# Hand-written order, a first batch on three queues, and q transposed by DMA, in a linear-attention and bilinear-FFN kernel

## The chip, the cores and the metric

The kernel runs on one core of one Trainium2 chip. The metric is the device time of one execution in microseconds (us). Every time quoted is the median of several runs. The span of a profile, from the first to the last instruction, is about 1.8 us shorter than the time of the same run; where spans and times are set beside each other, the text says so.

The engines are named as the profile names them: PE or TensorE (matmuls), PEld (its weight loads), DVE (VectorE), ACT (ScalarE), POOL (GpSimd), SP (the engine that here only issues transfers).

## The reference

Linear attention without a softmax, an RMS norm of each head's output, and then a bilinear feed-forward layer (FFN):

```python
# q, k, v: (8 batches, 8 heads, 576 tokens, 64), fp32; g_norm: (64,)
kv  = np.einsum('bhsd,bhse->bhde', k, v)
out = np.einsum('bhsd,bhde->bhse', q, kv)
rms = np.sqrt(np.mean(out * out, axis=-1, keepdims=True) + 1e-06)
x   = (out / rms * g_norm).transpose(0, 2, 1, 3).reshape(4608, 512)
# w_a, w_b: (512, 1536); w_out: (1536, 512)
result = ((x @ w_a) * (x @ w_b)) @ w_out          # (4608, 512), fp32
```

The kernels do all matmuls in bf16.

## The kernel before

A batch's attention makes 576 columns of `xt`, the transposed x. The FFN then eats `xt` in nine strips of 512 tokens. The attention of batch s+1 is woven into strip s. Only batches 0 and 1 have no earlier strip to hide in, which is why the first 75 us of the kernel differ from the rest.

All loads of q, k and v are issued by POOL and cast to bf16 in flight. DVE then reorders k and q so that TensorE can read them, and TensorE transposes q, five transposes to each of four pairs of heads:

```python
        def qT(self, p):                       # one pair of heads
            qt = self.t["qr"]                  # q, reordered by DVE
            ps = apsum.tile([128, S], BF16, name="q_ps", tag="at")
            for c in range(NCH + 1):           # 4 chunks of 128 tokens and one of 64
                nc.tensor.transpose(ps[:, c*128 : c*128+r], qt[0:r, c, hs, :], ident[0:r, 0:r])
            qs = asb_pool.tile([128, S], BF16, name="qs", tag="qs", bufs=5)
            nc.vector.tensor_copy(qs, ps)
        def xu(self, p, h):                    # x product of half h of the tokens, then its square
            ps = apsum.tile([128, HF], FP32, name="x_ps", tag="at")
            nc.tensor.matmul(ps, lhsT=self.kvd[:, p, :], rhs=self.qs[p][:, h*HF:(h+1)*HF], ...)
            nc.scalar.activation(sq, ps, AF.Square)
        def ss(self, p, h):                    # sum of squares, 1/rms, and the column of xt
            ps = apsum.tile([128, HF], FP32, name="s_ps", tag="at")
            nc.tensor.matmul(ps, lhsT=ones, rhs=self.sq[p, h], start=True, stop=True)
            nc.scalar.activation(rs, ps, AF.Abs_reciprocal_sqrt, bias=eps_t)
            nc.vector.scalar_tensor_tensor(out=xt[p][...], in0=self.x_ps[p, h],
                                           scalar=g_col, in1=rs, op0=ALU.mult, op1=ALU.mult)
# ... (kv products, loads)
    def ffn_ab(s, fc):                         # one of 12 units of a strip: 8 matmuls
        # 4 matmuls into a_ps, 4 into b_ps, 512 columns each
        nc.scalar.copy(a_sb, a_ps)
        nc.vector.tensor_mul(t, b_ps, a_sb)
# ... ffn_o: 4 groups of 12 output matmuls to each strip, then a store
    drain(Attn(0, loaded.pop(0), 2).slices())
    for fc in range(FC):
        ffn_ab(0, fc)
    drain(Attn(1, loaded.pop(1), 2).slices())
    for s in range(1, N_STRIP): ...            # strip s with the attention of batch s+1 woven in
```

(Cuts are marked with "..." here and in the code below.) There are four PSUM buffers under the tag "at", which kv, q, x and s share in turn, and four under the tag "f" for the FFN. An automatic scheduler chooses the final order on every engine.

## Time and profile before

| | before |
|---|---|
| time, median of 4 runs | 369.06 us (368.75 to 371.54) |
| span of the profiled run (its time: 371.11 us) | 369.4 us |
| period of a strip in the steady part | 36.9 us (strips 1 to 3), 37.1 us (strips 4 to 6) |
| end of batch 0's attention | 28.9 us |
| last a or b product of strip 0 ends | 56.7 us |

The profile cuts the span into 40 equal slices. A digit is the busy share of a slice in tenths; for PEclk it is the granted TensorE clock in tenths of full speed. These are three rows of the page of the kernel before:

```profile
PE   0588859999999999999999999999999999999994
...
PEclk9999885699999999999999999999999999999998
...
DMA  8999999999901511151001111100001111101023
```

TensorE is busy for 90% or more of every slice from the seventh to the last but one, but at full clock only from the ninth on (74 us). Until 102 us the transfers are full. The clock row reads 9 wherever the trace has no clock record, and the first record of this trace comes at 26.0 us. The matmuls tell the truth there: the 512-column ones took 631 ns before 25.5 us and 378 ns after 26 us. From 64 to 70 us, where the record reads 0.50, they took 631 ns again, so the 512-column matmuls before the first record ran at half clock.

Next, the table of stretches, of the kernel before. Its columns are the window, its length, the busy time of PE, PEld, DVE, ACT and POOL (with counts), the granted clock, the DMA share (the packets' times added up, over 16 engines: it passes 1 where packets overlap) and GB/s.

```profile
50.00:60.00 10.00, 5.77 (x33) 3.11 (x32) 3.77 (x7) 1.41 (x5) 3.97 (x6) 0.66 1.57 192
60.00:70.00 10.00, 8.95 (x37) 3.93 (x36) 5.49 (x13) 6.32 (x17) 5.41 (x7) 0.50 1.58 192
74.10:111.00 36.90, 36.90 (x202) 18.21 (x202) 18.05 (x32) 16.44 (x39) 8.14 (x10) 1.00 1.16 158
```

The last row is one period of the steady part: TensorE is busy in all of its 36.9 us, at full clock, and DVE and ACT in under half. There, only work taken off TensorE can help. The groups of instructions, by form, show what the transposes of q are. The columns are the count, the busy time, the mean ns of one, and the idle time before.

```profile
L175 DVE COPY qs<-q_ps 128x576 bf16<-128x576 bf16 x32 | 14.5, 452 | 13.9 <-PE q_ps L171 13.9
L171 PE MATMUL q_ps<-ident,qr 128*128 128x128 bf16 x128 | 14.3, 241 | 0.0
...
L171 PE MATMUL q_ps<-ident,qr 64*128 64x64 bf16 x32 | 6.7, 209 | 0.0
```

In the timeline of the start, TensorE stands twice before an FFN product. The bracket gives the idle time and what ended it.

```profile
38.41 0.38 PE L233 MATMUL b_ps<-xt_122,wb_t 128*128 128x512 bf16 x1 [2.17 <-DVE abt L243]
...
53.30 0.69 DVE L126 COPY kr<-kt 128x2048 bf16<-128x2048 bf16 x1 [6.21 <-DMA kt<-in_k_dram]
...
54.12 1.27 DVE L243 TENSOR_TENSOR abt<-b_ps,a_sb 128x512 bf16<-128x512 f32 x2
...
54.84 0.59 PE L233 MATMUL b_ps<-xt_122,wb_t 128*128 128x512 bf16 x1 [4.23 <-DVE abt L243]
```

The scheduler had put the reorder of a later batch's k (53.30) ahead of the product that TensorE needed (54.12), and that reorder waited 6.21 us for its load; the product ran only after it.

### The profile page before, as it was taken

Reading aid. Unit: us, or ns where it says so; the run is one execution under the profiler, and the core shown is the slowest. Engines: PE = TensorE matmul, PEld = TensorE weight load, DVE = VectorE, ACT = ScalarE, POOL = GpSimd, SP = SyncE. Lnnn points to the kernel's source line nnn. Section 1 sums busy time; section 2 is a strip of 40 time slices with the busy share of each in tenths; the row PEclk is TensorE's granted clock in tenths of the full one; section 3 lists DMA queues with packets and bytes.
Section 4 is the critical chain, followed back from the end, with each engine's and each line's share of the span. In section 5 each row is a group of like instructions: output and inputs, shape, how many; then the busy total and the mean of one; then the engine's idle time right before and its main releaser. Section 6 shows DMA issues by size and latency. Waiting matters only on the chain.

```text
span 369.4 us, 4627 instructions
## 1 busy us (share of the span) xinstructions
PE 341.7 (93%) x1744; PEld 163.8 (44%) x1744; DVE 149.7 (41%) x268; ACT 140.2 (38%) x320; POOL 57.6 (16%) x80
## 2 busy tenths in 40 slices
PE   0588859999999999999999999999999999999994
PEld 0333324444444444445444444444444444444441
DVE  1343535545543554355434543354335432222310
ACT  1164113633562356235523552355235522132210
POOL 7955635535000200020000000000000000000000
PEclk9999885699999999999999999999999999999998
DMA  8999999999901511151001111100001111101023
GB/s 96 177 196 192 165 193 192 191 191 204 210 32 30 69 51 31 29 73 49 28 30 28 28 30 29 30 28 29 30 28 30 28 28 30 29 28 59 28 58 85
DMA packets 51414, 28.61 MB, mean 77 GB/s; under 512 B 14528, under 2 KB 46784, under 8 KB 51392
## 3 DMA queue, kind: packets, MB, share of 16 engines
q0 software_dynamic: 45728, 18.88, 41.5%
q1 hardware_dynamic: 5664, 9.44, 9.2%
q8 instruction: 13, 0.21, 0.3%
q14 instruction: 9, 0.07, 0.1%
HBM read 37.75 MB, written 9.44 MB: 128 GB/s over the span
## 4 chain that ended last, share of the span: by engine, by line
PE 81%; DMA 11%; POOL 3%; ACT 2%; DVE 1%; issue 1%; POOLq 0%; ACTq 0%; DVEq 0%
PE o_ps L269 26%; PE a_ps L233 23%; PE b_ps L233 22%; DMA kt<-in_k_dram 4%; PE kv_ps L154 3%; PE q_ps L171 3%; DMA wa_t<-in_moe_w_a_dram 3%; DMA qt<-in_q_dram 2%; PE s_ps L194 2%; DMA vt<-in_v_dram 2%; PE x_ps L180 2%; POOL wb_t L67 1%; POOL wa_t L66 1%; ACT rs L196 1%; ACT sq L188 0%
## 5 line engine op out<-in xcount | busy, mean ns | idle before, releaser
L243 DVE TENSOR_TENSOR abt<-b_ps,a_sb 128x512 bf16<-128x512 f32 x108 | 74.4, 691 | 100.7 <-PE b_ps L233 94.2
L241 ACT CAST a_sb<-a_ps 128x512 bf16<-128x512 f32 x108 | 63.1, 586 | 108.1 <-PE a_ps L233 106.5
L269 PE MATMUL o_ps<-wo_t,abt 128*128 128x512 bf16 x432 | 98.6, 379 | 0.0
L233 PEld LDWEIGHTS <-wb_t 128*128 128x128 bf16 x432 | 42.8, 99 | 60.6 <-issue 13.3
L269 PEld LDWEIGHTS <-abt 128*128 128x128 bf16 x432 | 41.3, 98 | 46.7
L233 PEld LDWEIGHTS <-wa_t 128*128 128x128 bf16 x432 | 39.9, 99 | 39.0 <-issue 2.4
L233 PE MATMUL b_ps<-xt_122,wb_t 128*128 128x512 bf16 x108 | 42.4, 393 | 6.4 <-DVE abt L243 6.4
L233 PE MATMUL a_ps<-xt_122,wa_t 128*128 128x512 bf16 x108 | 42.6, 394 | 0.0
L233 PE MATMUL a_ps<-xt_123,wa_t 128*128 128x512 bf16 x108 | 41.9, 388 | 0.0
L233 PE MATMUL a_ps<-xt_125,wa_t 128*128 128x512 bf16 x108 | 41.2, 381 | 0.7 <-DVE xt_125 L198 0.5
L233 PE MATMUL b_ps<-xt_123,wb_t 128*128 128x512 bf16 x108 | 41.8, 387 | 0.0
L233 PE MATMUL b_ps<-xt_125,wb_t 128*128 128x512 bf16 x108 | 41.4, 384 | 0.0
L233 PE MATMUL b_ps<-xt_124,wb_t 128*128 128x512 bf16 x108 | 41.4, 384 | 0.0
L233 PE MATMUL a_ps<-xt_124,wa_t 128*128 128x512 bf16 x108 | 41.2, 381 | 0.2 <-DVE xt_124 L198 0.2
L188 ACT ACTIVATE sq<-x_ps 128x288 bf16<-128x288 f32 x64 | 26.1, 411 | 33.2 <-PE x_ps L180 32.8
L196 ACT ACTIVATE rs<-s_ps,eps_t 128x288 f32<-128x288 f32 x64 | 31.7, 498 | 1.9 <-PE s_ps L194 1.7
L154 PE MATMUL kv_ps<-vt,kr 128*128 128x128 bf16 (+1 forms) x160 | 20.2, 241 | 13.0 <-DMA vt<-in_v_dram 12.0
L280 DVE COPY o_sb<-o_ps 128x512 f32<-128x512 f32 x18 | 12.5, 692 | 38.3 <-PE o_ps L269 38.3
L278 ACT COPY o_sb<-o_ps 128x512 f32<-128x512 f32 x18 | 10.5, 586 | 45.4 <-PE o_ps L269 45.4
L154 PEld LDWEIGHTS <-kr 128*128 128x128 bf16 (+1 forms) x160 | 13.9, 105 | 24.4 <-issue 6.9
L86 POOL DMA_DIRECT2D vt<-in_v_dram x10 | 9.4, 941 | 77.1 <-PE kv_ps L154 71.6
L194 PE MATMUL s_ps<-sq,ones 128*128 128x288 bf16 x64 | 19.7, 308 | 1.8 <-ACT rs L196 0.7
(42 smaller groups left out, 196.4 us busy)
## 6 DMA issues: line engine op xcount, KB each, us to landing
out_dram<-o_sb SPq DMA_DIRECT2D x40, 128.0 KB, 2.4
out_dram<-o_sb SPq DMA_DIRECT2D x16, 256.0 KB, 2.2
kt<-in_k_dram POOLq DMA_DIRECT2D x6, 512.0 KB, 12.6
vt<-in_v_dram POOLq DMA_DIRECT2D x6, 512.0 KB, 10.7
qt<-in_q_dram POOLq DMA_DIRECT2D x6, 512.0 KB, 12.4
wa_t<-in_moe_w_a_dram POOLq DMA_DIRECT2D x6, 256.0 KB, 8.4
wb_t<-in_moe_w_b_dram POOLq DMA_DIRECT2D x6, 256.0 KB, 9.0
wo_t<-in_moe_w_out_dram POOLq DMA_DIRECT2D x2, 768.0 KB, 9.7
```

Of the source, the lines that this page charges most:

```text
L86: nc.gpsimd.dma_start(out=t[:, hs, 0:NCH, :], in_=src[b, hs, 0:SA, :].rearrange("h (sp c) d -> sp h c d", c=NCH),)
L154: nc.tensor.matmul(self.kv_ps[:, p, :], lhsT=kt[0:r, c, hs, :], rhs=vt[0:r, hs, c, :], start=(c == 0), stop=(c == NCH),)
L171: nc.tensor.transpose(ps[:, c * 128 : c * 128 + r], qt[0:r, c, hs, :], ident[0:r, 0:r])
L188: nc.scalar.activation(sq, ps, AF.Square)
L194: nc.tensor.matmul(ps, lhsT=ones, rhs=self.sq[p, h], start=True, stop=True)
L196: nc.scalar.activation(rs, ps, AF.Abs_reciprocal_sqrt, bias=eps_t)
L233: nc.tensor.matmul(ps, lhsT=w[:, kc, fc * 128 : (fc + 1) * 128], rhs=xt[kc][:, t0 : t0 + STRIP], start=(kc == 0), stop=(kc == KC - 1),)
L241: nc.scalar.copy(a_sb, a_ps)
L243: nc.vector.tensor_mul(t, b_ps, a_sb)
L269: nc.tensor.matmul(o_ps, lhsT=ab[s, fc][:, g * 128 : (g + 1) * 128], rhs=wo_t[:, fc, :], start=(fc == 0), stop=(fc == FC - 1),)
L278: nc.scalar.copy(o_sb, o_ps)
L280: nc.vector.tensor_copy(o_sb, o_ps)
```

## The change

Its intent: the scheduler is switched off and all engines run in the written order. The first batch's k and q arrive as fp32 on the queues of SP and ACT and are cast on the chip, while v stays on POOL. Every later batch's q goes, cast, through a bf16 scratch in DRAM and comes back by one transposing DMA, so TensorE no longer transposes it. Because the transposed q is in natural token order, stores become contiguous; batch 0, still transposed on TensorE, is put into natural order by a strided copy. Batch 0's attention is done in two halves of four heads. Dummy matmuls on zeros are to fill TensorE's idle time at the start.

```diff
+    ctx.enter_context(tc.manual_schedule())
 ...
+    for i in range(2):
+        hs = slice(i * HP, (i + 1) * HP)
+        load_heads(nc.sync, k0, k, 0, hs)        # fp32
+        load_heads(nc.scalar, q0, q, 0, hs)      # fp32
+        load_heads(nc.gpsimd, v0, v, 0, hs)      # bf16, cast in flight
 ...
+        scr = scr_pool.tile([NP, S, 2, D], BF16, name="scr", tag="scr")      # DRAM
+        for hl in range(2):
+            nc.gpsimd.dma_start(out=scr[:, :, hl, :].rearrange("p s d -> s p d"), in_=qv[hl])
 ...
+    def load_qT(t):
+        nc.sync.dma_start_transpose(out=qT[...], in_=t["scr"][...])
 ...
+    def dummies(n):
+        if n:
+            ps = apsum.tile([128, 512], FP32, name="w_ps", tag="at")
+            for _ in range(n):
+                nc.tensor.matmul(ps, lhsT=zt[:, 0:128], rhs=zt, start=True, stop=True)
 ...
-            nc.vector.tensor_copy(qs, ps)
+            nc.vector.tensor_copy(                          # natural token order, strided
+                qs[:, 0:SA].rearrange("p (s c) -> p c s", c=NCH),
+                ps[:, 0:SA].rearrange("p (c s) -> p c s", c=NCH),
+            )
 ...
+    dummies(13)
+    reorder(nc.vector, k0r, k0, slice(0, HP)); reorder(nc.scalar, q0r, q0, slice(0, HP))
+    at0.kv(0); at0.kv(1); at0.kv_out(slice(0, 2)); at0.qT(0); at0.qT(1)
+    at0.xu(0, 0); at0.xu(0, 1); dummies(2)
+    at0.ss(0, 0); at0.xu(1, 0); dummies(2)
+    at0.ss(0, 1); at0.xu(1, 1); dummies(2)
+    at0.ss(1, 0); dummies(2)
+    at0.ss(1, 1); dummies(4)
 ...      # second half: the same without dummies, the first matmuls of strip 0 woven in
+    for fc in range(2, FC):
+        ffn_ab(0, fc)
+    load_qT(loaded[1]); loaded[2] = load_b(2)
+    at1 = Attn(1); at1.take(loaded.pop(1))
+    for _ in at1.slices():
+        dummies(2)
 ...      # strips 1 to 8 as before, in written order
```

## The prediction

> **What bounds it now.** From 74 us on, TensorE alone: the per-stretch table has it busy throughout at full clock, DVE and ACT under half. The timeline gives the sum: a 512-column matmul every 0.216 us, so a strip of 512 tokens (144 of them) 31.1 us; one batch's attention adds 1.8 us of q transposes, 1.9 of kv, 2.0 of x and s: 36.7 against a measured period of 36.9. Before 74 us it is DMA and waits. DMA moves about 195 GB/s without pause until 100 us. In the chain of waits TensorE stands 2.2 us at 36 and 4.2 us at 50 behind a product on DVE, which, in order, sits on reorders of a later batch whose loads take 13 us. Batch 1's attention then runs at half clock (0.50 in 60-70 us). 369 = 69 (strip 1's start) + 8 x 31.1 + 6 x 5.7 + 10.4 (last products) + 4.9 (tail).
>
> **What changes.**
> 1. Steady part: q transposes of six batches leave TensorE, on the critical path: -10.8 us. Their DVE copies were slack.
> 2. Written order: no product behind a later batch's reorder: -6.4 us of stalls, about -2.5 us of half-clock matmuls, and part of the slow batch-1 attention.
> 3. First batch: fp32 k and q on the SP and ACT queues save serial issue (1.4 us a pair on POOL). [...] little gain. I estimate that the halves of attention 0 end near 15 and 24 us and strip 0 at 43 (88 matmuls left, 19 us).
> 4. Added: idle-filling dummies, mostly in waits. Batch 1's attention stays ACT-paced (0.41+0.50 us for each of 8 halves), about 13 us in all: strip 1 could start at 57.
> 5. DMA: q of a batch becomes 4608 packets of 128 bytes into DRAM. Traced ones take 32 ns against 60 ns of 512-byte ones, so an estimate of 6 us a batch instead of 3.4[...]. Batch 1 lands near 45-50 us, batch 2's v near 72-78, when attention 2 wants it at 73. I allow 1 us for the first and 2 us for the second. [...]
>
> **Sum.** 57 + 3 (late data) + 282 (8 x 31.1 + 6 x 3.9 + 10.4) + 4.9 = 347 us, 6% faster. Range 339 to 358. Chances: faster by over 2% 0.92, within 2% 0.06, slower 0.02.
>
> **What shows it right or wrong.** Step 1: strip periods of 35 us, no TensorE transposes after 25 us. Step 2: no TensorE idle over 1 us behind a product. Step 3: strip 0's last matmul near 43. Step 4: strip 1 starts at 57-60; granted clock above 0.9 in 40-60 us. Step 5: in the issue table scratch writes land within 12 us, transposes within 6; TensorE waits in strip 1 end on batch-2 loads.
>
> **What would make it wrong.** Each later transpose is issued only at its strip's start, behind the previous stores, and x needs it about 9 us later: beyond 9 us it stalls TensorE in five strips by the excess. Slower scratch writes push everything through 100 us. Less waiting in the first 60 us would bring 340.

The forecast's sum came to 347 us: 57 + 3 + 282 + 4.9. The 3 us for late data (1 for batch 1, 2 for batch 2) were the allowance.

## The result, and the profile after

| | before | after |
|---|---|---|
| time, median of 4 runs | 369.06 us (368.75 to 371.54) | 357.8 us (356.56 to 359.37) |
| ratio of fast runs | | 0.9688 [0.9632, 0.9743] |
| span of the profiled run | 369.4 us | 354.8 us |
| end of batch 0's attention | 28.9 us | 33.9 us |
| strip 0 ends | 56.7 us | 52.4 us |
| strip 1 starts | about 69.5 us (worked out, see below) | 66.5 us |
| strip period | 36.9 to 37.1 us | 35.0 us |

A ratio here is the mean time of one kernel's fast runs over that of the other's fast runs of the same rounds, so it is not quite the ratio of the medians that are quoted. The two profiled runs lie at opposite ends of their kernels' runs (371.11 and 356.56 us), so their spans differ by 14.6 us where the medians differ by 11.3. Part of the scatter goes with the clock: of the changed kernel's four runs the two with a mean granted clock of 0.975 and 0.976 took 356.73 and 356.56 us, the two with 0.960 and 0.961 took 359.37 and 358.86. So single traces are compared here by stage, and times by medians and intervals.

The same three rows of the page, of the changed kernel:

```profile
PE   6578997999989999999999999999999999999995
...
PEclk9559999999999999999999999999999999999999
...
DMA  8999999999939902990292032003100000011012
```

The low clock of the slices from 37 to 74 us is gone. The 5s from 9 to 27 us are no new loss by themselves: the kernel before ran at half clock there too, without a record that would show it. Here is the table of stretches of the changed kernel, by stage, with the columns as before:

```profile
9.00:14.00 5.00, 2.82 (x20) 1.75 (x20) 1.20 (x3) 0.52 (x2) 1.48 (x2) 0.58 1.35 243
14.00:26.00 12.00, 8.82 (x20) 2.09 (x19) 4.14 (x10) 4.77 (x10) 9.07 (x10) 0.50 1.45 196
26.00:34.00 8.00, 6.56 (x41) 3.44 (x42) 4.94 (x10) 3.87 (x10) 4.92 (x6) 0.95 1.92 178
34.00:52.30 18.30, 18.27 (x84) 8.01 (x82) 7.51 (x11) 6.92 (x12) 6.68 (x8) 1.00 1.44 187
52.30:66.50 14.20, 10.62 (x57) 4.67 (x57) 5.73 (x10) 6.93 (x18) 8.00 (x7) 1.00 1.74 174
66.50:103.70 37.20, 36.17 (x184) 17.20 (x183) 14.88 (x25) 15.43 (x33) 6.38 (x6) 1.00 1.25 130
138.70:173.70 35.00, 35.00 (x181) 16.93 (x180) 14.59 (x24) 15.24 (x33) 6.38 (x6) 1.00 0.75 98
```

The last row is a steady strip: 181 matmul records instead of 202, and 35.0 us instead of 36.9. Strip 0 (fourth row) runs without a gap at full clock. The sixth row is strip 1 and three products of strip 2. From strip 1's first product to strip 3's (66.55 to 138.32 us) it is 71.8 us, 1.8 more than two steady strips; two waits at the end of batch 2's attention are most of it:

```profile
102.55 0.28 PE L220 MATMUL s_ps<-sq,ones 128*128 128x288 bf16 x1 [0.74 <-ACT sq L214]
...
103.97 0.38 PE L269 MATMUL a_ps<-xt_146,wa_t 128*128 128x512 bf16 x1 [0.49 <-DVE xt_146 L224]
```

Batch 1's attention (fifth row) takes 14.2 us, with TensorE busy in 10.6 of them, a part of that in dummies.

The first half of batch 0's attention is the surprise. The timeline of the changed kernel there, PE, ACT and DVE:

```profile
9.34 0.38 PE L176 MATMUL kv_ps<-vt,k0r 128*128 128x128 bf16 x4 [2.63 <-DMA vt<-in_v_dram]
11.13 1.02 PE L176 MATMUL kv_ps<-vt,k0r 64*128 64x128 bf16 x6 [1.40 <-DMA vt<-in_v_dram]
...
12.89 1.29 DVE L197 COPY qs_195<-q_ps 128x512 bf16<-128x512 bf16 x1 [3.80 <-PE q_ps L193]
...
18.09 1.01 PE L155 MATMUL w_ps<-zt 128*128 128x512 bf16 x2 [0.15 <-DVE xt_143 L224]
...
19.15 0.40 PE L220 MATMUL s_ps<-sq,ones 128*128 128x288 bf16 x1
...
19.59 0.50 ACT L222 ACTIVATE rs<-s_ps,eps_t 128x288 f32<-128x288 f32 x1 [1.21 <-PE s_ps L220]
...
20.12 0.52 DVE L224 SCALAR_TENSOR_TENSOR xt_143<-x_ps,g_col,rs 128x288 bf16<-128x288 f32 x1 [2.09 <-ACT rs L222]
...
20.69 1.01 PE L155 MATMUL w_ps<-zt 128*128 128x512 bf16 x2 [0.15 <-DVE xt_143 L224]
```

Read it from 18.09 as a circle. Two dummies (w_ps) end at 19.10. Only then does the s product run: it stands behind them in the written order. ACT makes rs from it, DVE makes a column of xt, and the next dummies start 0.05 us after that column is done (20.69): they need the PSUM buffer that the xt product has just freed. A step of this circle takes 2.6 us. The kernel before, also at half clock, made its first four columns in steps of 1.0 to 1.2 us (they start at 20.84, 21.83, 22.82 and 24.04 us in its timeline).

The waits of the changed kernel, in us in total, times, and longest; these are the only waits of TensorE for data of the attention that reach 2 us:

```profile
PE kv_ps L176 <- DMA vt<-in_v_dram: 4.0, 2, 2.6
...
PE kv_ps L176 <- DVE kr L160: 2.1, 1, 2.1
```

The 6.4 us of waiting for an FFN product are gone. The table of DMA issues (count, KB each if listed, us from issue to landing, the median) and the chain of waits of the changed kernel close the picture:

```profile
scr<-in_q_dram POOLq DMA_DIRECT2D x14, 288.0 KB, 11.1
...
qT<-scr SPq DMA_TRANSPOSE x7, 5.1
```

```profile
145.51 2.70 PE o_ps L294 x12
...
180.50 2.70 PE o_ps L294 x12
```

The transposing DMAs landed 4.1 to 17.1 us after issue, the slow ones being the first two (17.1 and 11.4 us) while other loads were running. The chain runs on TensorE with one strip from 145.51 to 180.50, 34.99 us.

### Where the time came from, in the two profiled runs

| stage | before | after | difference |
|---|---|---|---|
| batch 0's attention ends | 28.9 | 33.9 | +5.0 |
| from there to the end of strip 0 (84 matmuls left in both) | 27.8 | 18.5 | -9.3 |
| batch 1's attention, until strip 1 runs | 12.8 | 14.2 | +1.4 |
| six strips with an attention woven in | 3 x 36.9 + 3 x 37.1 | 6 x 35.0 + 1.8 | -10.2 |
| strips 7 and 8 and the last outputs | 73.0 | 72.7 | -0.3 |
| tail after the last matmul | 4.9 | 3.8 | -1.1 |
| sum | | | -14.5 (the spans differ by 14.6) |

In the kernel before, the first products of strip 1 run among the steps of batch 1's attention, from 65.9 us on. Its start, 69.5 us, is therefore worked out: strip 7's first product, at 291.5 us, less six periods. The written order did save 9.3 us in strip 0, and batch 0's attention gave more than half of it back.

### The profile page after: what moved, and what is told of

It is laid out like the page before. It is cut to its first block, busy times and chain, and to the rows that moved or that the text cites. A ratio compares the mean times of both kernels' runs of the same rounds, so it can differ in the third digit from the quotient of the medians.

```text
span 354.8 us, 4305 instructions
## 1 busy us (share of the span) xinstructions
PE 335.8 (95%) x1649; PEld 156.2 (44%) x1649; DVE 134.2 (38%) x223; ACT 135.1 (38%) x278; POOL 59.2 (17%) x66
## 4 chain that ended last, share of the span: by engine, by line
PE 89%; DVE 3%; DMA 3%; ACT 2%; issue 1%; POOL 0%; ACTq 0%; DVEq 0%; POOLq 0%
PE o_ps L294 26%; PE b_ps L269 26%; PE a_ps L269 26%; PE kv_ps L176 4%; DMA vt<-in_v_dram 3%; PE s_ps L220 2%; PE x_ps L206 2%; PE w_ps L155 2%; ACT rs L222 1%; DVE xt_146 L224 1%; DVE xt_143 L224 0%; ACT sq L214 0%; DVE qs_282 L197 0%; DVE qs_195 L197 0%; DVE kr L160 0%
## 5 line engine op out<-in xcount | busy, mean ns | idle before, releaser
L269 PEld LDWEIGHTS <-wa_t 128*128 128x128 bf16 x432 | 42.2, 98 | 46.4 <-issue 2.8
L269 PE MATMUL a_ps<-xt_146,wa_t 128*128 128x512 bf16 x108 | 40.9, 379 | 0.8 <-DVE xt_146 L224 0.8
L269 PE MATMUL a_ps<-xt_143,wa_t 128*128 128x512 bf16 x108 | 40.9, 379 | 0.0
L269 PE MATMUL b_ps<-xt_145,wb_t 128*128 128x512 bf16 x108 | 40.9, 379 | 0.0
L269 PE MATMUL a_ps<-xt_145,wa_t 128*128 128x512 bf16 x108 | 40.9, 379 | 0.0
L269 PE MATMUL b_ps<-xt_146,wb_t 128*128 128x512 bf16 x108 | 40.9, 379 | 0.0
L269 PE MATMUL b_ps<-xt_144,wb_t 128*128 128x512 bf16 x108 | 40.9, 379 | 0.0
L269 PE MATMUL b_ps<-xt_143,wb_t 128*128 128x512 bf16 x108 | 40.9, 379 | 0.0
L269 PE MATMUL a_ps<-xt_144,wa_t 128*128 128x512 bf16 x108 | 40.9, 379 | 0.0
L125 POOL DMA_DIRECT2D scr<-in_q_dram x14 | 22.8, 1634 | 10.7 <-DMA wo_t<-in_moe_w_out_dram 7.0
L155 PE MATMUL w_ps<-zt 128*128 128x512 bf16 x45 | 17.4, 510 | 3.6 <-DVE eps_t L88 1.2
L70 POOL DMA_DIRECT2D kt<-in_k_dram x7 | 6.3, 893 | 87.0 <-DVE kr L161 85.2
L220 PE MATMUL s_ps<-sq,ones 128*128 128x288 bf16 x64 | 18.7, 293 | 1.1 <-ACT sq L214 0.7
## 6 DMA issues: line engine op xcount, KB each, us to landing
scr<-in_q_dram POOLq DMA_DIRECT2D x14, 288.0 KB, 11.1
wa_t<-in_moe_w_a_dram POOLq DMA_DIRECT2D x6, 256.0 KB, 10.8
```

The lines of the kernel that those rows point to most:

```text
L125: nc.gpsimd.dma_start(out=scr[:, :, hl, :].rearrange("p s d -> s p d"), in_=qv[hl])
L155: nc.tensor.matmul(ps, lhsT=zt[:, 0:128], rhs=zt, start=True, stop=True)
L269: nc.tensor.matmul(getattr(self, which), lhsT=w[:, kc, self.fc * 128 : (self.fc + 1) * 128], rhs=xt[kc][:, t0 : t0 + STRIP], start=(kc == ...
```

## The experiments

Two theories were set against each other for the slow first half. **Theory A**: the dummies set the pace, by their own time in TensorE's order and by taking a PSUM buffer out of the rotation. **Theory B**: the half clock sets the pace, with TensorE granted too little for want of early work, and more work early would cure it. Beside them stood the question which part of the change carries the gain: the written order, the queues, the dummies, or the transposing DMA.

Every kernel below had 5 timed rounds, 6 runs, all correct. Ratios are to the kernel before on the same chip (its medians: 369.4 us in the first set, 369.77 in the second, 369.75 in the third). "4th column" is the start of the fourth xt product, the end of the first half; "strip 0" is the start of its last b product.

| set | run | median us | ratio to before [95%] | 4th column | strip 0 |
|---|---|---|---|---|---|
| 1 | a0_control | 358.5 | 0.9699 [0.9665, 0.9733] | 25.51 | 52.35 |
| 1 | e1_no_mid | 357.1 | 0.9660 [0.9625, 0.9695] | 21.00 | 51.08 |
| 1 | e2_other_bank | 355.47 | 0.9623 [0.9591, 0.9654] | 22.55 | 51.55 |
| 1 | e4_no_late_dummies | 358.42 | 0.9685 [0.9655, 0.9715] | 25.50 | 52.83 |
| 2 | e5_one_queue | 359.4 | 0.9695 [0.9654, 0.9736] | 23.82 | 53.33 |
| 2 | e6_q_on_tensor | 371.47 | 1.0068 [1.0021, 1.0114] | 24.95 | 51.34 |
| 2 | e8_o_fills | 350.89 | 0.9488 [0.9455, 0.9520] | 25.35 | 53.42 |
| 2 | e9_best | 349.2 | 0.9423 [0.9383, 0.9463] | 22.32 | 51.39 |
| 3 | e3_no_dummies | 357.67 | 0.9664 [0.9638, 0.9691] | 21.20 | 51.38 |
| 3 | e11_warm | 357.26 | 0.9665 [0.9628, 0.9702] | 24.52 | 53.44 |
| 3 | e10_early_kv | 344.96 | 0.9341 [0.9315, 0.9367] | 21.77 | 52.16 |
| 3 | e12_both | 345.13 | 0.9324 [0.9299, 0.9349] | 21.78 | 53.58 |

### a0_control: the changed kernel again

No edit; it sets the scale for the others of its set.

> The changed kernel again, unaltered, as the yardstick of the other runs on this chip. All theories: about 357 us, ratio to the kernel before 0.969; in the trace the first half of batch 0's attention (last xt product) ends near 25 us, the second near 34, strip 1 starts near 66.5.

It gave 358.5 us (356.45 to 359.56), ratio 0.9699, like the first measurement (0.9688).

### e1_no_mid: no dummies inside batch 0's attention

```diff
-    dummies(2)      # four times, between the steps of the first half
-    dummies(4)      # once, after it
```

> The 12 dummy matmuls between the steps of batch 0's attention are taken out (the 13 ahead of it and those of batch 1 stay). Theory A, the dummies lie on the path (each pair lasts 1.0 us at half clock and takes one of four PSUM banks): a step shrinks from 2.6 to about 1.1 us, the first half ends at 19-20 us, strip 1 starts at 61-62 and the time falls by 4-5 us against the control. Theory B, the half clock is what is slow and the dummies only fill waits: the first half still ends at 24 us or later, the clock stays at half for longer into strip 0, and the time is equal or up to 3 us longer.

The step fell from 2.6 to 1.54 us and the fourth column came at 21.00 instead of 25.51. The clock was at half all the same, so theory A holds for the first half. But the time hardly moved: 357.1 us, with an interval that overlaps the control's. The gain was lost in the second half, which still ended at 33.6 us (34.9 in the control). The timeline of this kernel shows two causes: the casts of k for the second half ran slowly, and by the clock records the half clock lasted until 31.4 us, so that its steps took 1.33 us instead of 0.87.

```profile
20.98 3.31 POOL L125 DMA_DIRECT2D scr<-in_q_dram  x2 [0.59 <-DMA wa_t<-in_moe_w_a_dram]
...
21.44 1.66 DVE L160 CAST k0r<-k 128x1024 bf16<-128x1024 f32 x1
...
23.02 1.35 DVE L161 CAST k0r<-k 64x256 bf16<-64x256 f32 x1
```

The same two casts took 0.82 and 0.44 us in the changed kernel. Here they fall into the 3.31 us in which POOL issues the scratch writes. That they are slowed by it fits the other runs in part. The 64x256 cast took 1.35 or 1.36 us in all six runs in which it fell into that issue (e1, e2, e3, e9, e10, e12), and in each it ended within 0.1 us of the issue's end; elsewhere it took 0.27 to 0.45 us from fp32. The 128x1024 cast took 1.47 to 1.66 us in e1, e3 and e12, but 0.68 us in e2 and e9 and 0.81 us in e10, where it lay in the issue too. No run isolated it, so it stays a reading.

### e2_other_bank: dummies write into the other PSUM pool

```diff
-            ps = apsum.tile([128, 512], FP32, name="w_ps", tag="at")
+            ps = fpsum.tile([128, 512], FP32, name="w_ps", tag="f")
```

> All dummies stay, but write a bank of the feed-forward PSUM pool, idle at that time, and not one of the attention's four. Theory A1, it is the bank that the dummies take which serialises a step (x, then s, then the product that frees a bank): a step falls from 2.6 to about 1.5 us, the first half ends near 21 us, time -3 to -4 us against the control. Theory A2, it is TensorE time alone: a step stays above 2.2 us and the time within 1 us of the control. Theory B: no change.

The dummies now start beside the next x product instead of after the xt product. The timeline of this kernel:

```profile
19.37 0.52 DVE L224 SCALAR_TENSOR_TENSOR xt<-x_ps,g_col,rs 128x288 bf16<-128x288 f32 x1 [1.56 <-ACT rs L222]
19.39 0.40 PE L206 MATMUL x_ps<-qs,kvd 128*128 128x288 bf16 x1 [0.59 <-ACT rs L222]
...
19.58 1.06 PE L155 MATMUL w_ps<-zt 128*128 128x512 bf16 x2
```

The step is 2.08 us. So the circle of 2.6 us splits in two measured parts over the 1.54 us that are left without dummies: 0.52 us for the buffer, and 0.54 us for the dummies' own time that nothing hides. The steps of batch 1's attention, which have dummies too, fell from 1.17 to about 0.9 us, and strip 1 began at 65.59 instead of 67.84. The time is 355.47 us, ratio 0.9623: 0.8% better than the control.

### e3_no_dummies: none at all

```diff
-        if n:
+        if False:
```

> No dummy matmuls at all. Theory A (dummies on the path): steps of about 1.5 us at half clock, first half ends near 21 us; batch 1's attention gains 1.5 us but leaves the clock at half into strip 1; with the clock at half for longer everywhere the time is within 2 us of the control (ratio 0.965-0.975). If dummies were needed for the clock: +4 us or more (over 0.98).

357.67 us, ratio 0.9664 against the control's 0.9699 of another set. All 45 dummies together are worth nothing that these intervals show. What they cost in waiting they give back in clock, and the other way round: without them the first clock record comes at 32.4 us, strip 1 starts at 65.55 us instead of 67.84 (control), and then runs its first matmuls at half clock.

### e4_no_late_dummies: none in batch 1's attention

```diff
     for _ in at1.slices():
-        dummies(2)
+        pass
```

> The 2 dummies per step in batch 1's attention are taken out. Theory A: that attention's steps go from 1.17 to about 0.95 us (ACT-paced), strip 1 starts 1.5-2 us earlier, time -1 to -2 us. Theory B: TensorE is idle enough that its clock halves in strip 1's first matmuls, which gives 1-2 us back: no net change or slower by up to 2 us.

Strip 1 started 2.1 us earlier than in the control, at 65.77, and yet the time is the control's (358.42 us). The table of stretches of this kernel shows where it went:

```profile
57.35:65.77 8.42, 5.88 (x16) 1.71 (x17) 3.10 (x6) 6.99 (x17) 3.52 (x5) 0.50 1.76 173
65.77:71.00 5.23, 5.23 (x14) 1.81 (x13) 1.73 (x3) 1.26 (x3) 2.67 (x2) 0.51 1.64 174
```

In the attention the clock fell to half, and strip 1's first 5.2 us ran at half clock, which costs 2.6 us. Here dummies do buy the clock, at about the price that it is worth. In the traces of the two kernels every clock record reads 0.5 or 1.0, and all recorded stretches of one clock, but for the last of each trace, which its end cuts, have lengths that are multiples of the shortest, 3.41 us: in the kernel before 13.65, 3.41, 10.24, 17.07 and 296.96 us, in the changed one 3.41, 17.07 (from 9.8 to 26.8 us) and 327.68 us. The half clock of this run, 0.51 in the mean from 57.4 to 71.1 us, lasted about 13.7 us, which fits.

### e5_one_queue: the first batch by POOL alone, cast in flight

```diff
-    k0 = first.tile([128, H, NCH + 1, D], FP32, name="k0")      # q0 alike
+    k0 = first.tile([128, H, NCH + 1, D], BF16, name="k0")
 ...
-        load_heads(nc.sync, k0, k, 0, hs)
-        load_heads(nc.scalar, q0, q, 0, hs)
+        load_heads(nc.gpsimd, k0, k, 0, hs)
         load_heads(nc.gpsimd, v0, v, 0, hs)
+        load_heads(nc.gpsimd, q0, q, 0, hs)
```

> The first batch is loaded by POOL alone, cast in flight and half by half as before (k, v, q), all else as changed. Theory C, the start is late because v shares the DMA engines with fp32 k and q: v's first half lands near 9 us and not 10-12, the first kv product runs 1-3 us earlier, the first half of the attention ends 1-2 us earlier, time -1 to -2 us against the control's 358.5. Theory D, the three queues are worth having: first products later, time +1 to +3 us. Prediction's reading [...]: within 1 us.

359.4 us, ratio 0.9695 against the control's 0.9699. Three queues and on-chip casts are worth nothing that can be measured here. With POOL alone the kv products even started sooner (8.44 us against 10.17), with v issued ahead of q instead of beside it. Theory C's earlier start came, then, but not its gain in time. Its reason, that v shares the DMA engines with k and q, was the author's reading: the runs show the order and the start, not which engine moved what.

### e6_q_on_tensor: later q back on TensorE

The scratch and the transposing DMA go; later batches' q is loaded by POOL and transposed on TensorE, as before, in the written order, with all the rest of the change kept.

```diff
-        scr = scr_pool.tile(...)                 # and its two writes
+        t["q"] = qkv_pool.tile([128, H, NCH + 1, D], BF16, name="qt", tag="q")
+        load_heads(nc.gpsimd, t["q"], q, b, slice(0, H))
 ...
-        nc.sync.dma_start_transpose(...)
+        pass
 ...
-            for p in range(NP):
-                self.q[p] = t["qT"][:, p, :]
+            self.qr = qkv_pool.tile([128, NCH + 1, H, D], BF16, name="qr", tag="qr", bufs=1)
+            reorder(nc.vector, self.qr, t["q"], slice(0, H))
 ...
+                    if h and p + 1 < NP:
+                        self.qT(p + 1)           # and qT(0) after the kv products
```

> The later q go back to TensorE: loaded cast, reordered on DVE, 20 transposes a batch; no scratch, no transposing DMA; written order and first batch as changed. Prediction's step 1: TensorE transposes cost 1.8 us in each of six strips on the path, and 1.8 us or more in batch 1's attention, so the strip period is 36.8 us against 35.0 and the time +11 to +14 us against the control, about 370 us. Rival, transposes are hidden in waits once the order is written by hand: +5 us or less.

371.47 us, ratio 1.0068 [1.0021, 1.0114]: not faster than the kernel before at all. The table of stretches of this kernel has the old period, and the chain of waits confirms it (142.42 to 179.26):

```profile
140.00:176.84 36.84, 36.84 (x202) 18.20 (x200) 19.83 (x34) 15.59 (x33) 4.81 (x6) 1.00 0.51 77
```

```profile
142.42 2.59 PE o_ps L287 x12
...
179.26 2.59 PE o_ps L287 x12
```

So the net gain of the change is that of the transposing DMA. By the ratios that is 3.7% of the time before, 13.6 us; by the period six strips at 1.84 us give 11.0, and strip 1, before which batch 1's attention now holds transposes, starts 1.6 us later than in the control (69.48 against 67.84). That is 12.6 us, and the difference to 13.6 is within the intervals. The rest of the change nets nothing in e6. It is 4.3 us ahead of the kernel before at the end of strip 0 (52.4 against 56.7 us), but batch 1's attention then takes 17.1 us against 12.8, with its transposes and with strided copies on DVE. These copies belong to the natural token order, and e6 keeps them for every batch, which the kernel before does not have (DVE is busy for 19.83 us of a strip against 18.05). A version with the old copies and stores and only the written order was not tried.

### e8_o_fills: real work in place of dummies

Strip 0's 48 output matmuls, which the change did in strip 1, now fill batch 1's attention in place of its dummies, five to a step. The transposing DMA of batch 2 is issued earlier.

```diff
+    load_qT(loaded[2])
 ...
+    o0 = (x for g in range(NG) for x in ffn_o_steps(0, g))   # one matmul of strip 0's output at a time
     for _ in at1.slices():
-        dummies(2)
+        step(o0, 5)
+    for _ in o0:
+        pass
 ...
-        o_at = [5, 7, 9, 11] if s == 1 else [2, 5, 8, 11]
+        o_at = [] if s == 1 else [2, 5, 8, 11]
```

> Batch 1's attention is filled with the 48 output matmuls of strip 0 (10.4 us of needed work) in place of 20 dummies; strip 1 then has no output products. If TensorE there only waits for ACT (theory A: the fill is free), that attention grows from 14 to 16-17 us, strip 1 shrinks by 10-12 us, and the time falls by 8-9 us to about 350. If the steps are limited by something that the fill also uses (ACT copies, PSUM), a step grows to over 1.8 us and the gain is under 4 us.

350.89 us, ratio 0.9488. Against the control's ratio that is 2.1% of the time before, 7.8 us, of the 10.4 us (48 x 0.2157) that moved.

### e9_best: e8, the other bank, and half of the strided copies on ACT

```diff
-            ps = apsum.tile([128, 512], FP32, name="w_ps", tag="at")
+            ps = fpsum.tile([128, 512], FP32, name="w_ps", tag="f")
 ...
-            nc.vector.tensor_copy(
+            cp = nc.scalar.copy if p % 2 else nc.vector.tensor_copy
+            cp(
```

(together with the edits of e8)

> e8 with the dummies in the other pool's bank and every second strided q copy of batch 0 on ACT. Theory A adds the 3 us of the bank experiment and up to 1 us per half for the copies: 345-348 us, against about 350 without. If the clock's phase eats it, as part of the gain was eaten when the dummies were removed: within 1 us of e8.

349.2 us, ratio 0.9423, about 0.7% below e8; their intervals just overlap. The first half's steps are 2.08 us, as in e2. The strided 128x512 copy takes 1.29 us on ACT, no less than on DVE (1.29 us in the changed kernel); the contiguous 128x576 copy of the kernel before took 0.45 us on DVE.

### e11_warm: 29 dummies at the head instead of 13

```diff
-    dummies(13)
+    dummies(29)
```

> 29 dummies ahead of batch 0's data and not 13, so that TensorE does not stand idle for 3 to 5 us before v lands and its clock need not fall back to half. Theory B, half clock is most of the slow first half: dummies of 0.22 us each in place of 0.43, a step falls from 2.6 to about 1.7 us, the first half ends near 20-21 us and not 25, the time falls by 3-5 us against the control (ratio 0.957-0.962). Theory A, dummies and bank pace it whatever the clock: a step stays above 2.3 us, first half ends after 24, time within 1 us of the control (0.970), or longer if the extra dummies delay kv.

This is theory B's own test. The clock was full until 14.4 us instead of 11.0 in the control, and the kv products and transposes were quicker (ten transposes 0.99 us against 1.48). Then, in the first steps, it fell to half for 20.5 us, although TensorE had stood idle for no more than 1.23 us at a time since its first dummies. The steps took 2.6 us as before, the fourth column came at 24.52, and the time is 357.26 us, no different from the others. An early warm clock did not last through steps that wait, so the cure that theory B proposes fails. How much of a step of 2.6 us is due to the half clock stays open: in no run did the first half's steps with their dummies run at full clock. (In batch 1's attention of the control, at full clock and with two dummies a step, a step took 1.17 us.)

### e10_early_kv and e12_both: batch 1's kv products inside strip 0

e10 is e9 with the reorder of batch 1's k and its kv products moved into strip 0, and with the transposing DMAs of batches 1 and 2 and batch 2's loads written ahead of strip 0's third unit; e12 is e10 with 29 dummies at the head.

```diff
-    for fc in range(2, FC):
-        ffn_ab(0, fc)
 ...
-    at1.take(loaded.pop(1))
-    for _ in at1.slices():
-        dummies(2)
+    g1 = at1.slices()
+    for fc in range(2, FC):
+        ffn_ab(0, fc)
+        if fc == 7:
+            at1.take(loaded.pop(1))       # reorder of k, on DVE
+        if fc == 9:
+            step(g1)                      # the kv products
 ...      # then the output matmuls of strip 0 beside g1, as in e8
```

> The filled version with the dummies in the other bank, and batch 1's k reorder and kv products placed inside strip 0 (after its 8th and 10th unit), where k and v have landed. The 2.3 us wait of TensorE for the reorder goes and the clock has no gap to fall in: 3-4 us less than the version without, about 345 us, ratio 0.930-0.935. If k or v land later than I read (38 and 41 us), DVE or TensorE waits in strip 0 and the gain is under 1 us.

> The same with 29 dummies at the head. Theory B adds 2-4 us to it: about 342 us, ratio 0.922-0.928. Theory A: no difference from the version with 13.

e10 took 344.96 us, ratio 0.9341; e12 345.13 us, ratio 0.9324, the same within their intervals. The table of stretches of e10 shows batch 1's attention with TensorE busy all the time, with real work, and in the stretch before it the kv products inside strip 0:

```profile
34.00:52.20 18.20, 18.20 (x97) 8.66 (x96) 8.04 (x13) 6.26 (x12) 6.41 (x6) 1.00 1.43 186
52.20:65.30 13.10, 13.10 (x69) 6.61 (x68) 5.99 (x12) 7.61 (x18) 7.42 (x7) 1.00 1.72 173
```

In the changed kernel DVE's reorder of k began only after the last product of strip 0 and TensorE waited 2.1 us for it. These two versions beat both kernels: about 6.6% under the one before and, by ratios of different sets, 3.7% under the change.

## Why the prediction was right or wrong

The measured 357.8 us lies in the range of 339 to 358, at its very end, and the sign was right. That it lies inside at all is luck: two of the four runs (358.86 and 359.37 us) and the control's median (358.5) lie outside. The predicted 347 was 10.8 us too low, and the gain about half of the forecast. Point by point:

- **Step 1, right.** Transposes leave TensorE: period 35.0 us, exactly the predicted 31.1 + 3.9, and 12.0 us in six strips where 10.8 were forecast. e6 puts them back and gets 36.84.
- **Step 2, right in the main.** The two stalls behind a product (6.4 us) and the half clock after them are gone. From the end of batch 0's attention on, strip 0 took 18.5 us instead of 27.8. The part of the slow batch-1 attention that was to go as well did not: 14.2 us against 12.8.
- **Step 3, wrong.** "I estimate that the halves of attention 0 end near 15 and 24 us and strip 0 at 43": they ended at 25.3 and 33.9, and strip 0 at 52.4. The first half carries the error: it was off by 10.3 us, while the second took 8.6 us where 9 had been allowed. The first half's 25.3 us are kv products that wait 4.0 us for v and end at 12.1, transposes and two strided copies of 1.29 us at half clock until the first steps, and four columns, which start at 17.5, 20.1, 22.7 and 24.8 us. "Little gain" from the queues was right (e5).
- **Step 4, half right.** That the dummies would lie "mostly in waits" was wrong in batch 0's attention, where each step paid 1.06 us for them (e1, e2). The clock in 40 to 60 us was 1.00, as predicted. At what share of busy time the clock rises or falls, these traces do not show: from 14 to 26 us TensorE was busy for 8.82 of 12.0 us (73%), with no gap above 0.7 us, and the clock stayed at half (0.50); in batch 1's attention, with 10.62 of 14.2 us (75%) and a gap of 2.1 us, it stayed full (1.00). Batch 1's attention took 14.2 us, as predicted (43 to 57), but it started 9.4 us late.
- **Step 5, wrong only in what it feared.** Scratch writes landed in 11.1 us in the median, though up to 21.3; transposes in 5.1. By the packet records the quickest transpose moved its 2304 packets (0.59 MB) in 2.34 us, 253 GB/s. But they began 1.3 us after the issue, and it landed 4.1 us after it. The five later ones moved at 183 to 253 GB/s and landed after 4.1 to 6.5 us; the first two, beside other loads, moved at 47 and 91 GB/s and landed after 17.1 and 11.4 us. The loads, scratch writes and transposes of later batches were hidden: in the steady strip the DMA share was 0.75 and TensorE was busy in all of the 35.0 us. No batch was late: batch 1's q was there at 51.4 us and wanted at 57.3. Most of the 1.8 us that strips 1 and 2 lost are waits for ACT and DVE at the last steps of batch 2's attention (0.74 and 0.49 us), which the change starts late in strip 1; none is a wait for loads of batch 2. The feared stall in five strips did not come.

The sum, term by term, in us of the span:

| term | predicted | measured | difference |
|---|---|---|---|
| attention 0's halves end | 24 | 33.9 | +9.9 |
| rest of strip 0 | 19 | 18.5 | -0.5 |
| batch 1's attention | 14 | 14.2 | +0.2 |
| late data or other delays | 1 + 2 | 1.8 | -1.2 |
| strips 1 to 8 | 282 | 282.6 | +0.6 |
| tail | 4.9 | 3.8 | -1.1 |
| sum | 346.9 | 354.8 | +7.9 |

The mechanism of the gain was right; one term was mis-sized, the end of batch 0's attention, at 24 instead of 33.9 us. The remaining 3 us are of bookkeeping: the terms are those of a span, and the time is 1.8 us longer than its span; and the profiled run was 1.2 us quicker than the median. The prediction's own decomposition of the time before has the same flaw: its terms add up to 367.3, not 369.

What the runs show in place of the failed step is a little more than "dummies are dear". Taking them away made the first half 4.3 to 4.5 us shorter (e1, e3) and gained nothing significant, because the second half then ran at half clock, with slow casts, and ended only 1.3 us sooner. Over all the runs of the table the fourth column moved between 21.0 and 25.5 us, and the last b product of strip 0 only between 51.1 and 53.6 us (in e10 and e12 with 2.0 us of kv products in it). The prediction should have set its 24 us beside the trace that it had: the kernel before finished this attention at 28.9 us, at half clock until 26 us, with all its loads on one queue.

It did so in steps of 1.0 to 1.2 us, where e1, without dummies and at half clock too, needs 1.54. Both kernels have the x and s products in the same order, but they wait for different things. From the timeline of the kernel before:

```profile
20.86 0.40 PE L194 MATMUL s_ps<-sq,ones 128*128 128x288 bf16 x1 [0.35 <-ACT rs L196]
...
21.41 0.40 PE L180 MATMUL x_ps<-qs,kvd_118 128*128 128x288 bf16 x1 [0.16 <-DVE xt_122 L198]
```

And from that of e1:

```profile
16.95 0.40 PE L206 MATMUL x_ps<-qs,kvd 128*128 128x288 bf16 x1 [0.59 <-ACT rs L222]
...
17.51 0.40 PE L220 MATMUL s_ps<-sq,ones 128*128 128x288 bf16 x1 [0.16 <-DVE xt L224]
```

In e1 x waits until rs has read the s buffer, and s until the column has read the x buffer, as if only three of the four "at" buffers were in turn. The code says which is missing: `kv_ps` is allotted once for both halves of batch 0 and written again in the second half, so it holds a buffer through the first. In the kernel before, all kv products are done before the first x product. e3 agrees: batch 1's attention, in the same order, without dummies and at half clock, but with `kv_ps` done at its start, takes 0.99 us a step, against 1.54 in batch 0's first half of the same run. A second `kv_ps` was not tried; from three steps of 0.55 us an estimate of its worth in the first half is 1.7 of the 5.0 us. Open, too, is what slows DVE's casts under POOL's scratch issue.

## What to carry to other kernels

When a change replaces a scheduler's order by a written one, set each stage of the plan beside the same stage in the old trace before costing it: the old schedule may be better in places, and here one stage lost more than half of what another had gained. Filler work was not free here where it took a buffer (0.52 us a step, e2) or a slot (0.54 us) that the critical chain needed, and the clock that it bought was worth no more than it cost (e3, e4); real work moved into the same hole (e8, e10) paid 2 to 4%. Where one engine is busy all the time, as TensorE was here, take work off that engine first: taking the transposing DMA out again lost all of the net gain (e6).
